# Idle matmuls in TensorE's waits of the front, and two weight units begun early in place of one

## The chip, the cores and the metric

The kernel runs on one core of a Trainium2 chip. The metric is the time of one execution on the device in microseconds (us), as the median of several runs; the profile is of one further execution, with the span of the core's instructions beside its time.

## The reference

For 4 batches and 8 heads, with 576 positions of 64 elements, attention is the sum of two parts: a local one, softmax over the keys within 3 positions, and a dense one between means over 4 neighbouring positions (144 of them), repeated fourfold. The result, as 2304 tokens of 512 elements, goes through two feed-forward layers.

```python
q_d, k_d, v_d = (t.reshape(B, H, Sd, 4, D).mean(axis=3) for t in (q, k, v))
out_up = np.repeat(sm_attn(q_d, k_d, v_d), 4, axis=2)
scores = np.where(np.abs(pos[:, None] - pos[None, :]) < 4, scale * q @ k.T, -1e9)
out_local = softmax(scores) @ v
x = (out_up + out_local).transpose(0, 2, 1, 3).reshape(B * S, H * D)     # 2304 x 512
x = (silu(x @ w_gate) * (x @ w_val)) @ w_out                              # 512 -> 1536 -> 512
h = x @ w2_in                                                             # 512 -> 2048
return (h * clip(h + 3, 0, 6) / 6) @ w2_out                               # 2048 -> 512
```

## The kernel before

The tokens are worked in five blocks (`BLOCKS = [8, 6, 8, 8, 6]`, in units of 64 tokens). The kernel has two stages. In the **front** (to about 65 us) `first_batch` computes the attention of the first batch, whose tokens are block 0 with 64 left over, in five tiles of 122 tokens (the last of 88). A tile i passes through `scores(i)` (TensorE writes `fS`), `norm(i)` (VectorE takes the maxima `fnm`, ScalarE the exponentials `held` with their sums `fsm`, VectorE the reciprocal and the multiply), `trans(i)` (TensorE transposes into `fPT`, ScalarE copies to `turned`) and `values(i)` (TensorE writes `fO`, VectorE adds the dense part on the way out: `fxf`). `put_cols` then splits the tile into a high part (ScalarE) and a low part (VectorE) in `xr`, the moving operand of the feed-forward layers, kept as two fp32r numbers for each value.

From then on, in the **dense** stage, `run_unit` goes through the weight units of each block: G0, G1, V0, V1, G2, G3, V2, V3 and so on, then the products with `w_out` (`aO`), then H and `aP` for the second layer. A unit of kind G, V or H is 12 matmuls of up to 512 columns into a bank `mm`, of which there are two, so that V0 needs the bank of G0, and G2 that of V0. The bank of G0 is read by ScalarE's silu (`sl`); that of V0 by VectorE's product `sl0` (L950), which G2 therefore waits for. Only unit 0 (`HALVES = 1`) is cut in two column ranges, of 244 and 268 columns, so that its first range can run as soon as two tiles are done, between the matmuls of the later tiles.

A weight unit passes through five steps, each started some units ahead (`LR, LD, LA, LB, LS = 8, 6, 5, 4, 3`): `load_raw` (SyncE's queue loads `w64`, four buffers), `decode_a` (ScalarE, `top`), `decode_b` (VectorE, `w32`, three buffers of two units each), `split_unit` for each pair (ScalarE the high part and VectorE the low part of `wr`, three buffers), and in block 0 a write of the decoded pair to memory (`kept`), issued on ScalarE's queue. Blocks 1 to 4 load `kept` into the same buffers as `w32`. In block 0 the attention of the next batches runs on VectorE beside the matmuls: products `pr` of `q` and `k`, reductions, products with `v`, and sums `o`, which TensorE transposes (`px`).

The order on each engine comes from a scheduler that goes by the program's order and its own estimate of when things are ready; instructions under `keep_in_program_order` are held in the order of the code. In the front, matmuls without use (`fill`, L431, 512 columns of zeros) already stand in the waits ahead of the first tiles.

```python
ps = bank("mm", f"p{kind}{bi}_{f}", 2)[:, :nt]
cols = [slice(0, nt)]
if i < HALVES:
    cols = [slice(0, 244), slice(244, nt)]
```

Of the kernel before, what the change touches and what calls it, by code (L numbers as in the profile page):

```python
# [12 lines left out]
BF16 = mybir.dt.bfloat16  # L13
# [8 lines left out]
P = 128  # L22
# [7 lines left out]
CUTS = [[3, 2], [2, 2, 2, 2], [3, 2, 3], [3, 3], []]  # L30
LR, LD, LA, LB, LS = 8, 6, 5, 4, 3
WARM = 14
HALVES = 1
CLOAD = (0, 4)


# [9 lines left out]
def tile_kernel(  # L46
# [12 lines left out]
    nc = tc.nc  # L59
# [9 lines left out]
    NC = DM // P  # L69
# [18 lines left out]
    def bank(tag, name, bufs=1):  # L88
        return pp.tile([P, 512], F32, tag=tag, name=name, bufs=bufs)
# [8 lines left out]
    ident = cp.tile([P, P], F32, name="ident")  # L98
# [169 lines left out]
    def put_cols(bi, col, xv):  # L268

        if bi not in xr:  # L270
            xr[bi] = sp.tile([P, NC, 2, UMAX * UT], F32R, tag="xr", name=f"xr{bi}")
        dst = xr[bi][:, :, :, col:col + xv.shape[2]]
        nc.scalar.activation(dst[:, :, 0], xv, AF.Copy)  # L273
        nc.vector.tensor_tensor(dst[:, :, 1], xv, dst[:, :, 0].bitcast(F32), op=ALU.subtract)
# [42 lines left out]
    def first_batch():  # L317

        QT = 122
# [4 lines left out]
        with tc.tile_pool(name="fp", bufs=1) as fp:  # L324
# [72 lines left out]
            def values_of(i):  # L397
                return vw[i][:, i % 2].rearrange("p (h d) -> p h d", h=H)
# [32 lines left out]
            def fill(ps, n):  # L431

                for _ in range(n):
                    tc.keep_in_program_order(nc.tensor.matmul(ps, idle[:, :P], idle, start=True, stop=True))

            def load_T(w, c):
                src = qn[w, c // 2]
                for th in range(2):
                    tag = ("acc0", "acc1", "acc2")[turn[0] % 3]
                    turn[0] += 1  # L440
                    ps = bank(tag, f"fT{w}{c}{th}")
                    fill(ps, 2)
                    ps = ps[:, :S // 2]
                    for t in range(3):
                        tc.keep_in_program_order(nc.tensor.transpose(
                            ps[:, t * TT:(t + 1) * TT],
                            src[:, 3 * th + t, c % 2 * 2:c % 2 * 2 + 2].rearrange("j h d -> j (h d)"),
                            ident[:TT, :TT],
                        ))
                    if w == "q":  # L450
                        nc.vector.tensor_scalar(
                            qT[:, c, th * S // 2:(th + 1) * S // 2], ps, 0.125, None, op0=ALU.mult
                        )
                    else:
                        nc.scalar.activation(kT[:, c, 3 + th * S // 2:3 + (th + 1) * S // 2], ps, AF.Copy)
# [67 lines left out]
            def size(i):  # L523
                return min(QT, S - QT * i)
# [55 lines left out]
            def trans(i):  # L580
                n = size(i)
                w_ = n + 6
                pT[i] = turned[:WK, i % 2, :NC * 2 * QT].rearrange("p (c a s) -> p c a s", c=NC, a=2)
                for hh in range(2):
                    ps = bank(f"acc{2 + hh}", f"fPT{i}_{hh}")[:, :4 * QT]
                    ps = ps.rearrange("p (c a s) -> p c a s", c=2, a=2)
                    for m in range(4):
                        nc.tensor.transpose(
                            ps[:w_, m // 2, m % 2, :n], pe[i][:n, 2 * hh + m // 2, m % 2, :w_], ident[:n, :n]
                        )  # L590
                    to = pT[i][:w_, 2 * hh:2 * hh + 2, :, :n]
                    nc.scalar.activation(to, ps[:w_, :, :, :n], AF.Copy)

            def values(i):
                n = size(i)
                w_ = n + 6
                t0 = QT * i
                po = bank(("pa", "px")[i % 2], f"fO{i}")[:, :NC * QT].rearrange("p (c s) -> p c s", c=NC)
                for c in range(NC):
                    for par in range(2):  # L600
                        rows = slice(par * D, par * D + D)
                        nc.tensor.matmul(
                            po[rows, c, :n], values_of(i)[:w_, 2 * c + par, :], pT[i][:w_, c, par, :n],
                            start=True, stop=True,
                        )

                xf = sp.tile([P, UMAX * UT], F32, tag="sl", name=f"fxf{i}", bufs=3)[:, :NC * QT]
                xf = xf.rearrange("p (c s) -> p c s", c=NC)[:, :, :n]
                cuts = [0]
                head = -t0 % 4  # L610
                if head:
                    cuts.append(head)
                cuts.append(head + (n - head) // 4 * 4)
                if cuts[-1] < n:
                    cuts.append(n)
                for a, e in zip(cuts, cuts[1:]):
                    j0, m = (t0 + a) // 4, e - a
                    if m % 4 == 0 and (t0 + a) % 4 == 0:
                        nc.vector.tensor_tensor(
                            xf[:, :, a:e].rearrange("p c (j t) -> p c j t", t=4),  # L620
                            po[:, :, a:e].rearrange("p c (j t) -> p c j t", t=4),
                            od[:, :, j0:j0 + m // 4, None].to_broadcast([P, NC, m // 4, 4]), op=ALU.add,
                        )
                    else:
                        nc.vector.tensor_tensor(
                            xf[:, :, a:e], po[:, :, a:e], od[:, :, j0:j0 + 1].to_broadcast([P, NC, m]), op=ALU.add,
                        )
                a = 0
                while a < n:
                    bi = max(m for m in range(NB) if starts[m] * UT <= t0 + a)  # L630
                    e = min(n, starts[bi + 1] * UT - t0)
                    put_cols(bi, t0 + a - starts[bi] * UT, xf[:, :, a:e])
                    a = e
# [21 lines left out]
            down_values(1)  # L655
            next(ahead)
            trans(0)
            down_trans(3)
            down_values(2)
            scores(2)  # L660
            prefetch(5 - LR)
            norm(1)
            down_values(3)
            values(0)
            for i in range(1, NT):
                next(ahead, None)
# [44 lines left out]
    def values_d(po, par, vd, h, pt):  # L711
        for kh in range(2):
            nc.tensor.matmul(  # L713
                po[par * D:par * D + D], vd[:, kh, h, :], pt[:, kh, :], start=kh == 0, stop=kh == 1
            )

    first_batch()


# [204 lines left out]
    def run_unit(i):  # L924
        kind, f, bi = units[i]
        nt = BLOCKS[bi] * UT
        r = split.pop(i)
        if kind in "GVH":
            ps = bank("mm", f"p{kind}{bi}_{f}", 2)[:, :nt]
            x = xr[bi] if kind != "H" else state["x2"]  # L930
            cols = [slice(0, nt)]
            if i < HALVES:
                cols = [slice(0, 244), slice(244, nt)]
            for cs in cols:
                for part in (HIGH, LOW):
                    for c in range(NC):
                        for a, b_ in part:
                            nc.tensor.matmul(  # L938
                                ps[:, cs], r[:, a, c], x[:, c, b_, cs],
                                start=part is HIGH and a == c == 0, stop=part is LOW and c == NC - 1,  # L940
# [17 lines left out]
        else:  # L958
# [12 lines left out]
            for part in (HIGH + LOW,) if last else (HIGH, LOW):  # L971
                for e in range(nb):
                    ps = state["acc"][e]
                    ps = ps[:, :nt] if kind == "O" else ps
# [160 lines left out]
```

## Time and profile before

| | |
|---|---|
| median of 3 runs | 967.26 us (966.04 to 967.92) |
| profiled execution, its own time | 962.81 us |
| its span | 961.0 us |
| mean granted TensorE clock | 0.99 |
| TensorE busy | 934.2 us (97%) |
| VectorE busy | 733.5 us (76%) |
| ScalarE busy | 506.7 us (53%) |
| bytes moved by DMA | 160.79 MB |

The busy share of TensorE is that of both stages together: in the first 77.5 us of the span it is busy for 61.80 us, with a mean granted clock of 0.89, and after that nearly always. A granted clock of 1.00 is 2.4 GHz and one of 0.50 is 1.2 GHz. Times in the rows are microseconds from the start of the span.

### The profile page before, as it was taken

How to read it: one execution, taken by the hardware profiler on the slowest of the kernel's cores; microseconds unless marked ns; L12 is line 12 of the kernel's file. 1: busy time of each engine (PE TensorE's matmuls, PEld its weight loads, DVE VectorE, ACT ScalarE, POOL GpSimd, SP SyncE). 2: the span in 40 equal slices, each digit the busy share in tenths (PEclk: the TensorE clock that was granted, in tenths of full speed). 3: DMA queues.
4: the chain of work that ended last, by engine and by line, in shares of the span. 5: the costliest groups of instructions: out<-in, count | busy, mean ns of one | idle time of the engine just before them, and what ended most of it. 6: DMA issues, size and time to landing. Idle time of an engine off the chain costs nothing.

```text
span 961.0 us, 12930 instructions
## 1 busy us (share of the span) xinstructions
PE 934.2 (97%) x4800; PEld 789.1 (82%) x4800; DVE 733.5 (76%) x1067; ACT 506.7 (53%) x945; POOL 111.0 (12%) x115
## 2 busy tenths in 40 slices
PE   8779999999999999999999999999999999999997
PEld 5567888777799988878888778888888888999996
DVE  7689967799889979999664799996347994445652
ACT  4676667876554577543244764443335444444542
POOL 5742000000053300015410000000000000000000
PEclk9789999999999999999999999999999999999999
DMA  8999999466699823359962212462323223434331
GB/s 207 170 271 316 327 341 351 155 209 226 238 287 270 176 72 108 123 189 237 203 139 96 78 66 85 160 216 90 108 88 105 92 88 112 152 132 132 119 123 33
DMA packets 116339, 160.79 MB, mean 167 GB/s; under 512 B 61868, under 2 KB 83756, under 8 KB 116276
## 3 DMA queue, kind: packets, MB, share of 16 engines
q1 hardware_dynamic: 67892, 131.41, 42.3%
q0 software_dynamic: 43488, 10.72, 11.1%
q10 hardware_dynamic: 4896, 17.83, 4.7%
q8 instruction: 38, 0.62, 0.3%
q14 instruction: 25, 0.20, 0.1%
HBM read 137.29 MB, written 22.54 MB: 166 GB/s over the span
## 4 chain that ended last, share of the span: by engine, by line
PE 83%; DVE 11%; ACT 3%; issue 2%; DMA 1%; SPq 0%; ACTq 0%; DVEq 0%
PE pH L938 17%; PE aP L980 16%; PE pG L938 15%; PE aO L980 15%; PE pV L938 15%; DVE wr L237 2%; DVE pv L809 1%; ACT held L560 1%; PE pS L863 1%; DVE xf L838 1%; DVE h L954 1%; PE pO L713 1%; DMA k<-in_k_dram 1%; DVE pv L813 1%; PE pPT L706 1%
## 5 line engine op out<-in xcount | busy, mean ns | idle before, releaser
L237 DVE TENSOR_TENSOR wr<-w,wr 128x1024 fp32r<-128x1024 f32 x170 | 207.5, 1221 | 121.6 <-ACT wr L236 121.3
L236 ACT ACTIVATE wr<-w 128x1024 fp32r<-128x1024 f32 x170 | 179.7, 1057 | 132.4 <-issue 63.1
L938 PE MATMUL pH<-x,wr 128*128 128x512 f32 (+1 forms) x960 | 212.4, 372 | 0.0
L980 PE MATMUL aP<-wr,gH 128*128 128x512 f32 x864 | 211.4, 395 | 0.3 <-ACT gH L955 0.3
L938 PEld LDWEIGHTS pH<-x,wr 128*128 128x128 f32 x960 | 173.0, 188 | 25.1 <-issue 2.5
L980 PEld LDWEIGHTS aP<-wr,gH 128*128 128x128 f32 x864 | 159.6, 188 | 35.1 <-issue 2.7
L938 PE MATMUL pG<-xr,wr 128*128 128x512 f32 (+3 forms) x732 | 156.5, 368 | 3.8 <-ACT xr L273 3.2
L938 PE MATMUL pV<-xr,wr 128*128 128x512 f32 (+1 forms) x720 | 153.4, 368 | 0.0
L980 PE MATMUL aO<-gV,wr 128*128 128x512 f32 (+1 forms) x720 | 152.7, 368 | 0.0
L938 PEld LDWEIGHTS pG<-xr,wr 128*128 128x128 f32 x732 | 133.4, 190 | 21.4 <-ACT xr L273 3.8
L938 PEld LDWEIGHTS pV<-xr,wr 128*128 128x128 f32 x720 | 130.9, 188 | 16.7
L980 PEld LDWEIGHTS aO<-gV,wr 128*128 128x128 f32 x720 | 130.8, 188 | 16.7
L953 ACT ACTIVATE h<-pH,consts 128x512 f32<-128x512 f32 (+1 forms) x80 | 51.5, 644 | 59.7 <-PE pH L938 59.4
L944 ACT ACTIVATE sl<-pG 128x512 f32<-128x512 f32 (+1 forms) x60 | 33.3, 556 | 72.9 <-PE pG L938 72.8
L955 ACT ACTIVATE gV<-sl 128x512 fp32r<-128x512 f32 (+1 forms) x60 | 35.0, 583 | 65.6 <-DVE sl L950 65.5
L955 ACT ACTIVATE gH<-h 128x512 fp32r<-128x512 f32 (+1 forms) x80 | 46.9, 586 | 32.1 <-DVE h L954 31.8
L954 DVE SCALAR_TENSOR_TENSOR h<-h,pH 128x512 f32<-128x512 f32 (+1 forms) x80 | 50.5, 631 | 14.8 <-ACT h L953 14.2
L772 DVE TENSOR_TENSOR pr<-q,k 128x1792 f32<-128x1792 f32 x27 | 54.5, 2020 | 8.3 <-DMA k<-in_k_dram 8.1
L956 DVE TENSOR_TENSOR gH<-h,gH 128x512 fp32r<-128x512 f32 (+1 forms) x80 | 50.5, 632 | 10.4 <-ACT gH L955 10.0
L214 ACT ACTIVATE top<-w 128x512 f16<-128x512 bf16 x68 | 52.1, 788 | 11.0 <-DMA w<-in_moe_w_out_dram 2.9
L809 DVE TENSOR_TENSOR pv<-sc,v 128x1792 f32<-128x1792 f32 x27 | 54.6, 2022 | 0.5
L775 DVE TENSOR_REDUCE sc<-pr 128x28 f32<-128x1792 f32 x27 | 54.3, 2013 | 0.2
(125 smaller groups left out, 758.4 us busy)
## 6 DMA issues: line engine op xcount, KB each, us to landing
w<-kept SPq DMA_DIRECT2D x136, 512.0 KB
kept<-w ACTq DMA_DIRECT2D x34, 512.0 KB
w<-in_moe_w_out_dram SPq DMA_DIRECT2D x28, 512.0 KB
w<-in_moe_w_in_dram SPq DMA_DIRECT2D x16, 512.0 KB
w<-in_moe_w_gate_dram SPq DMA_DIRECT2D x12, 512.0 KB
w<-in_moe_w_val_dram SPq DMA_DIRECT2D x12, 512.0 KB
out_dram<-os SPq DMA_DIRECT2D x16, 256.0 KB
dnq<-in_q_dram POOLq DMA_DIRECT2D x24, 144.0 KB, 7.4
```

The costliest lines, as they stand in the source:

```text
L214: behind(nc.scalar.activation(halves(top[i % 2], 2, F16)[:, :, 1], h3.bitcast(BF16), AF.Copy))
L236: behind(nc.scalar.activation(r[:, :, 0], s, AF.Copy))
L237: behind(nc.vector.tensor_tensor(r[:, :, 1], s, r[:, :, 0].bitcast(F32), op=ALU.subtract))
L772: nc.vector.tensor_tensor(pr, qt[:, a:a + SUB, None, :].to_broadcast([P, SUB, W, D]), win(kt, a, SUB), op=ALU.mult)
L775: nc.vector.tensor_reduce(sc[:, a:a + SUB], pr, axis=AX.X, op=ALU.add)
L809: nc.vector.tensor_tensor(pr, pe[:, a:a + SUB, :, None].to_broadcast([P, SUB, W, D]), win(vt, a, SUB), op=ALU.mult)
L938: nc.tensor.matmul(ps[:, cs], r[:, a, c], x[:, c, b_, cs], start=part is HIGH and a == c == 0, stop=part is LOW and c == NC - 1,)
L953: nc.scalar.activation(h, ps, AF.Relu, scale=1 / 6, bias=half1[:, 0:1])
L954: nc.vector.scalar_tensor_tensor(h, h, 1.0, ps, op0=ALU.min, op1=ALU.mult)
L955: nc.scalar.activation(g[:, 0, :nt], h, AF.Copy)
L956: nc.vector.tensor_tensor(g[:, 1, :nt], h, g[:, 0, :nt].bitcast(F32), op=ALU.subtract)
L980: nc.tensor.matmul(ps, **one, start=f_ == 0 and a == b_ == 0, stop=f_ == nf - 1 and b_ == 1,)
```

## The change

A new function `fill_late` issues n matmuls of 128x256 bf16 elements, the identity by itself, whose result is not used, into the bank that the next step of the tile writes to. `trans(i)` calls it ahead of its first transposes with 0, 6, 10, 12 and 0, and `values(i)` ahead of its matmuls with 0, 0, 0, 4 and 6: 38 in all. Second, two units (G0 and G1) are cut in column ranges, not one, and the first range has 366 columns (three tiles) in place of 244 (two tiles).

```diff
--- before.py
+++ after.py
@@ -30,7 +30,8 @@
 CUTS = [[3, 2], [2, 2, 2, 2], [3, 2, 3], [3, 3], []]
 LR, LD, LA, LB, LS = 8, 6, 5, 4, 3
 WARM = 14
-HALVES = 1
+FILL_T, FILL_V = (0, 6, 10, 12, 0), (0, 0, 0, 4, 6)
+HALVES = 2
 CLOAD = (0, 4)
 
 
@@ -432,6 +433,14 @@
 
                 for _ in range(n):
                     tc.keep_in_program_order(nc.tensor.matmul(ps, idle[:, :P], idle, start=True, stop=True))
+
+            turner = ident.bitcast(BF16)
+
+            def fill_late(ps, n):
+                for _ in range(n):
+                    tc.keep_in_program_order(
+                        nc.tensor.matmul(ps[:, :2 * P], turner[:, :P], turner, start=True, stop=True)
+                    )
 
             def load_T(w, c):
                 src = qn[w, c // 2]
@@ -582,8 +591,10 @@
                 w_ = n + 6
                 pT[i] = turned[:WK, i % 2, :NC * 2 * QT].rearrange("p (c a s) -> p c a s", c=NC, a=2)
                 for hh in range(2):
-                    ps = bank(f"acc{2 + hh}", f"fPT{i}_{hh}")[:, :4 * QT]
-                    ps = ps.rearrange("p (c a s) -> p c a s", c=2, a=2)
+                    ps = bank(f"acc{2 + hh}", f"fPT{i}_{hh}")
+                    if not hh:
+                        fill_late(ps, FILL_T[i])
+                    ps = ps[:, :4 * QT].rearrange("p (c a s) -> p c a s", c=2, a=2)
                     for m in range(4):
                         nc.tensor.transpose(
                             ps[:w_, m // 2, m % 2, :n], pe[i][:n, 2 * hh + m // 2, m % 2, :w_], ident[:n, :n]
@@ -595,7 +606,9 @@
                 n = size(i)
                 w_ = n + 6
                 t0 = QT * i
-                po = bank(("pa", "px")[i % 2], f"fO{i}")[:, :NC * QT].rearrange("p (c s) -> p c s", c=NC)
+                po = bank(("pa", "px")[i % 2], f"fO{i}")
+                fill_late(po, FILL_V[i])
+                po = po[:, :NC * QT].rearrange("p (c s) -> p c s", c=NC)
                 for c in range(NC):
                     for par in range(2):
                         rows = slice(par * D, par * D + D)
@@ -930,7 +943,7 @@
             x = xr[bi] if kind != "H" else state["x2"]
             cols = [slice(0, nt)]
             if i < HALVES:
-                cols = [slice(0, 244), slice(244, nt)]
+                cols = [slice(0, 366), slice(366, nt)]
             for cs in cols:
                 for part in (HIGH, LOW):
                     for c in range(NC):
```

The scheduler gives another order for this program. The first place is VectorE in the front, tiles 3 and 4: the digit behind a name is the tile, `fnm4` are the maxima of tile 4, `fsm3` the sums of tile 3, `held` the multiply of tile 3, `xr0` the low part of tile 1, `w32` a decode, `fxf2` the addition of tile 2. Before:

```order
L558 TENSOR_REDUCE fnm4_764<-fS4_0_765 88x4
L558 TENSOR_REDUCE fnm4_764<-fS4_1_766 88x4
L569 TENSOR_SCALAR fsm3_697<-fsm3_697 122x8
L570 RECIPROCAL fsm3_697<-fsm3_697 122x8
L571 TENSOR_TENSOR held_229<-held_229,fsm3_697 122x1024
L274 TENSOR_TENSOR xr0_678<-fxf1_742,xr0_678 128x4x122
L223 SCALAR_TENSOR_TENSOR w32_2_726<-w64_3_394,top1_161 128x512
L619 TENSOR_TENSOR fxf2_807<-fO2_798,tmp_262 128x4x120
```

With the change:

```order
L578 TENSOR_SCALAR fsm3_703<-fsm3_703 122x8
L579 RECIPROCAL fsm3_703<-fsm3_703 122x8
L567 TENSOR_REDUCE fnm4_780<-fS4_0_781 88x4
L567 TENSOR_REDUCE fnm4_780<-fS4_1_782 88x4
L275 TENSOR_TENSOR xr0_678<-fxf1_748,xr0_678 128x4x122
L224 SCALAR_TENSOR_TENSOR w32_2_732<-w64_3_394,top1_161 128x512
L580 TENSOR_TENSOR held_229<-held_229,fsm3_703 122x1024
L632 TENSOR_TENSOR fxf2_823<-fO2_814,tmp_262 128x4x120
```

The sums and the reciprocal of tile 3 come ahead of the maxima of tile 4, and the multiply `held` goes behind the `xr0` and the decode.

The second place is VectorE at the dense start, from the low part of the second weight pair (`wr4`) on: `pr1_0` and `sc1_0` are the next batch's first chunk, `sl0_0` is the product of silu(G0) and V0. Before:

```order
L237 TENSOR_TENSOR wr4_929<-w32_4_885,wr4_929 128x2x512
L772 TENSOR_TENSOR pr1_0_0_1087<-q1_0_890,k1_0_892 128x1792
L775 TENSOR_REDUCE sc1_0_1086<-pr1_0_0_1087 128x28
L223 SCALAR_TENSOR_TENSOR w32_6_959<-w64_7_789,top1_161 128x512
L223 SCALAR_TENSOR_TENSOR w32_8_1012<-w64_8_882,top0_159 128x512
L772 TENSOR_TENSOR pr1_0_4_1251<-q1_0_890,k1_0_892 128x1792
L950 TENSOR_TENSOR sl0_0_921<-sl0_0_921,pV0_0_961 128x512
L237 TENSOR_TENSOR wr6_982<-w32_6_959,wr6_982 128x2x512
```

With the change:

```order
L238 TENSOR_TENSOR wr4_967<-w32_4_923,wr4_967 128x2x512
L785 TENSOR_TENSOR pr1_0_0_1137<-q1_0_928,k1_0_930 128x1792
L224 SCALAR_TENSOR_TENSOR w32_6_1009<-w64_7_805,top1_161 128x512
L224 SCALAR_TENSOR_TENSOR w32_8_1062<-w64_8_920,top0_159 128x512
L788 TENSOR_REDUCE sc1_0_1136<-pr1_0_0_1137 128x28
L785 TENSOR_TENSOR pr1_0_4_1301<-q1_0_928,k1_0_930 128x1792
L224 SCALAR_TENSOR_TENSOR w32_8_1062<-w64_9_963,top1_161 128x512
L238 TENSOR_TENSOR wr6_1032<-w32_6_1009,wr6_1032 128x2x512
L963 TENSOR_TENSOR sl0_0_959<-sl0_0_959,pV0_0_1011 128x512
```

The reduction `sc1_0` goes behind two decodes, and a further decode (of raw unit 9) and the subtraction `wr6` stand ahead of `sl0_0`. On ScalarE the silu of G0 comes behind the first decoding steps of raw units 7 and 8 there, and that of G1 behind the write-out `kept3` and the step of unit 9; before, both silus stood ahead of them. On TensorE 3 matmuls of G0's first range stand ahead of `fO3`, where 2 stood ahead of `fO2`, 6 ahead of `fO3` and 1 ahead of `fO4`; the rest of G0 and all of G1 come behind `fO4` in both.

The third place is ScalarE near the end of block 0, around the write-out `kept31`; `h` and `gH` belong to the H units 12 and 13, `wr` and `top` to weight units. Before:

```order
L273 ACTIVATE xr1_875<-xf12_2455 128x4x64
L953 ACTIVATE h0_13_2527<-pH0_13_2513,consts_101 128x512
L955 ACTIVATE gH0_12_2500<-h0_12_2501 128x512
L236 ACTIVATE wr62_2510<-w32_62_2485 128x2x512
L955 ACTIVATE gH0_13_2526<-h0_13_2527 128x512
L229 DMA kept31_156<-w32_62_2485 128x1024
L214 ACTIVATE top1_161<-w64_65_2462 128x512
```

With the change:

```order
L274 ACTIVATE xr1_913<-xf12_2505 128x4x64
L215 ACTIVATE top0_159<-w64_64_2474 128x512
L966 ACTIVATE h0_12_2551<-pH0_12_2537,consts_101 128x512
L237 ACTIVATE wr62_2560<-w32_62_2535 128x2x512
L230 DMA kept31_156<-w32_62_2535 128x1024
L968 ACTIVATE gH0_12_2550<-h0_12_2551 128x512
L966 ACTIVATE h0_13_2577<-pH0_13_2563,consts_101 128x512
L215 ACTIVATE top1_161<-w64_65_2512 128x512
L215 ACTIVATE top0_159<-w64_66_2532 128x512
```

The write-out `kept31` now stands directly behind `wr62`, ahead of `gH0_12` and `h0_13`. In the same stretch TensorE's `px13` stands right behind unit pH14 and no longer behind three matmuls of pH15, and on VectorE the subtraction `wr64` stands ahead of the decode of raw unit 66, with the same set of work ahead of `o`. GpSimd's order is the same, and SyncE's loads stand in the same order up to unit 66.

## Rows read from the trace of the kernel before

**Rows 1.** TensorE by stretch of the span: us, busy (instructions), granted clock, DMA share, GB/s

```profile
49.20:52.40 3.20, 3.18 (x44) 1.00 1.32 253
55.20:58.50 3.30, 3.30 (x23) 0.50 1.35 186
65.50:68.60 3.10, 3.10 (x14) 0.50 1.02 399
77.50:961.00 883.50, 872.37 (x4318) 1.00 0.55 163
```

**Rows 2.** Waits of TensorE after 77.5: line, releaser, us in total, times, longest

```profile
PE px L829 <- DVE o L815: 3.4, 5, 2.4
```

**Rows 3.** Chain of waits into 77.51: start, us, what

```profile
62.02 7.51 DMA k<-in_k_dram
...
76.86 0.61 DVE sl L950
...
77.51 0.50 PE pG L938
```

**Rows 4.** Timeline of TensorE: start, us, instruction, count, [idle before, releaser]

```profile
5.60 0.59 PE L434 MATMUL fTq<-idle 128*128 128x512 bf16 x2
...
49.22 1.10 PE L602 MATMUL fO<-turned,vw 128*64 128x122 f32 x16 [1.97 <-ACT turned L592]
50.25 1.05 PE L588 MATMUL fPT<-ident,held 122*128 122x122 f32 x8
...
55.10 0.72 PE L938 MATMUL pG<-xr,wr 128*128 128x244 f32 x2 [2.70 <-ACT xr L273]
55.74 1.89 PE L602 MATMUL fO<-turned,vw 128*64 128x122 f32 x16
...
71.20 5.71 PE L938 MATMUL pV<-xr,wr 128*128 128x512 f32 x24
```

**Rows 5.** Timeline of VectorE in the front, tiles 2 to 4

```profile
52.74 0.99 DVE L558 TENSOR_REDUCE fnm<-fS 88x4 f32<-88x376 f32 x2
...
54.40 1.22 DVE L571 TENSOR_TENSOR held<-held,fsm 122x1024 f32<-122x1024 f32 x1
55.55 0.66 DVE L274 TENSOR_TENSOR xr<-fxf,xr 128x488 fp32r<-128x488 f32 x1
...
57.68 0.66 DVE L619 TENSOR_TENSOR fxf<-fO,tmp 128x480 f32<-128x480 f32 x1 [0.88 <-PE fO L602]
```

**Rows 6.** Timeline of VectorE at the dense start

```profile
66.32 1.23 DVE L237 TENSOR_TENSOR wr<-w,wr 128x1024 fp32r<-128x1024 f32 x1 [0.50 <-ACT wr L236]
69.64 2.03 DVE L772 TENSOR_TENSOR pr<-q,k 128x1792 f32<-128x1792 f32 x1 [2.10 <-DMA k<-in_k_dram]
...
73.64 1.28 DVE L223 SCALAR_TENSOR_TENSOR w<-w,top 128x512 int32<-128x512 int32 x2
```

**Rows 7.** Timeline of ScalarE, front and dense start

```profile
59.47 1.07 ACT L592 ACTIVATE turned<-fPT 128x488 f32<-128x488 f32 x2
...
67.90 0.60 ACT L944 ACTIVATE sl<-pG 128x512 f32<-128x512 f32 x1
...
71.74 1.41 ACT L214 ACTIVATE top<-w 128x512 f16<-128x512 bf16 x2
...
74.36 1.07 ACT L236 ACTIVATE wr<-w 128x1024 fp32r<-128x1024 f32 x1 [0.96 <-DVE w L223]
```

**Rows 8.** Timeline of TensorE, VectorE and ScalarE's queue around 253.75

```profile
253.75 0.41 PE L829 MATMUL px<-ident,o 128*128 128x128 f32 x2 [2.36 <-DVE o L815]
...
251.45 0.69 DVE L223 SCALAR_TENSOR_TENSOR w<-w,top 128x512 int32<-128x512 int32 x1 [2.09 <-ACT h L953]
...
244.36 0.33 ACTq L229 DMA_DIRECT2D kept<-w  x1
```

**Rows 9.** DMA queue q10 from 242.3 to 248 and 248 to 251.4: packets, MB, share

```profile
q10 hardware_dynamic: 2, 0.00, 0.2%
...
q10 hardware_dynamic: 144, 0.52, 37.7%
```

## The prediction

> **What bounds the kernel now.** I read TensorE's windows first. From 77.50 us to the end of the span it is busy 872.37 of 883.50 us at a granted clock of 1.00 [rows 1]; its longest waits there are 3.4 us in five pieces ahead of `px` [rows 2]. From the dense stage on TensorE is the bound, so the end moves with two things: when the unbroken run of matmuls that begins with unit G2 (77.51) can start, and what happens to the waits behind it. Ahead of 77.51 TensorE waits for others. So I read second the chain of waits into 77.51 [rows 3]: the load of `k` for the next batch lands 7.51 us after its issue at 62.02; VectorE then makes two products, a reduction and two decodes of weights, and behind them `sl`, the product of silu(G0) and V0, which frees the bank that G2 writes to. VectorE had idled 2.10 us for `k` [rows 6]. What happens to TensorE ahead of that is not on the path, unless it moves the issue of `k` or comes later than this cover.
>
> Third, TensorE's clock in the front. After the wait of 2.70 us that ends at 55.10 [rows 4] the granted clock is 0.50 from 55.20 to 58.50, the level of 1.2 GHz, and again from 65.50 to 68.60; after the wait of 1.97 us that ends at 49.22 [rows 4] it is 1.00 until 52.40 [rows 1]. The 16 matmuls of `fO` took 1.10 us at the one level and 1.89 at the other [rows 4].
>
> **The change part by part.**
>
> *The 38 fills.* None has run in this form. The nearest row is the old fill, two of 512 columns in 0.59 us, 0.3 us each at most [rows 4]; by half the columns I take 0.15 us, and 0.3 as the upper end. Ten of them (1.5 us) stand ahead of tile 2's transposes, which followed `fO1` at once at 50.25 [rows 4]. They and the scores of tile 4 come 1.5 us later; VectorE, in its new order, asks for these scores only behind tile 3's reciprocal at 54.4 [rows 5], so that is hidden. Twelve stand between `fO2` (ends at 55.74 + 1.10 = 56.8) and tile 3's transposes: 1.8 us, so these start at 58.6 and end at 59.4, or 60.2 at half clock; ScalarE took them at 59.47 [rows 7]. So it is 0 to 0.7 us late there (2.5 with 0.3 us for each), and with it the rest of the front. The cover is VectorE's 2.10 us of idling for `k`; only at the upper price 0.4 us would come through.
>
> What the fills may win is the half clock at 55.20, 0.79 us of `fO2` [rows 4]. On the path it is worth nothing, since VectorE's order turns around: the multiply `held` of tile 3 now stands behind two reductions (0.99), an `xr` (0.57) and a decode (0.64), and so ends at 55.62 + 2.2 = 57.8 us; the addition that empties `fO2` used to start at 57.68 [rows 5] and starts behind it, at about the same time. Cost of the fills 0; ends -0.8 (if `fO2`'s gain is passed on to the load of `k`) and +0.4.
>
> *The split of G0 and G1.* The columns are the same; G1's 12 matmuls become 24. A matmul of 512 columns takes 5.71/24 = 0.24 us [rows 4] and a shorter one no more, so the extra is 0 to 2.9 us. The cover is ScalarE: silu0, which started at 67.90 behind the table load, now also stands behind two decodes, which took 1.41 us [rows 7]. So silu0 starts at about 69 and V0 at 69.5, whenever G0 is done before 69. Cost 0. Should it miss by a us, V1 still ends before `sl0` is ready.
>
> *The order at the dense start.* Here the change costs. On VectorE `sl0` stood directly behind the second product; now a decode (`w32_8`'s second half) and the subtraction `wr6` stand between. A decode takes 1.28/2 = 0.64 us, such a subtraction 1.23 us [rows 6]: G2 starts at 77.51 + 1.87 = 79.4. Lower end 0, if VectorE came 1.9 us earlier, for which `k` would have to land earlier; upper end more than 1.87 if ScalarE's half of `wr6` is late. That half started at 74.36 [rows 7] and now comes behind silu1 and `qdT`; it may slip by the 1.9 us without being late.
>
> *The clock at the new wait.* silu1 stands on ScalarE behind the write-out `kept3`, which waits for the decode w7 (69.64 + 2.03 + 0.64 = 72.3 [rows 6]), and behind one decode of 0.7: V1 runs from 73.7 to 76.6. Then G2 waits about 2.6 us. That lies between the 1.97 that left the clock up and the 2.70 that was followed by a fall. A fall costs half of 3.3 us [rows 1], 1.65, since TensorE is the bound from there. Both ends, 0 and 1.65, stay open; I take 0, narrowly, since a fall that comes already in the pause of 1.2 us ahead of V1 is hidden.
>
> *The wait at 253.75.* TensorE waited 2.36 us for `o`, and VectorE, just before, 2.09 us to begin the decode w66 [rows 8]. The view names ScalarE's `h`; but this decode writes to the buffer from which `kept31` is written out. That write was issued at 244.36 [rows 8], and its queue (q10) moved next to nothing until 248 and 0.52 MB from there to 251.4 [rows 9]: the wait is for the write. ScalarE's new order issues `kept31` right behind `wr62`, ahead of two `gH` and an `h`, so ahead of the loads that crowded it. Then VectorE's 2.09 us go. `px` now also stands three matmuls (0.71 us) earlier in TensorE's row. With VectorE as late as TensorE the wait left is 2.36 - 2.09 + 0.71 = 0.98, so 1.4 us come back; if VectorE keeps its time (its two pieces of work were brought forward, not added), all 2.36. I take 1.9, between the two; ends 0 and 2.36.
>
> **Sum.** 0 (fills) + 0 (split) + 1.9 (order) + 0 (clock) - 1.9 (write-out) = 0.0 us. It is made against the profiled execution, 962.81 us (span 961.0); the runs' median of 967.26 is 0.46% more, and the change of 0.0 is carried over to it: 967.3 us. 0.2%, about what a measurement of this kernel can tell from no change, is 1.93 us.
>
> The page "DMA: Bandwidth & Descriptors" of the Trainium skill (section "Anatomy of one DMA — SWDGE (gpsimd) path") gives a transfer about 2.0 us and its bytes over 436e3 per us. For `k`, 576 KB, that would be an estimated 3.4 us; the trace shows 7.51 [rows 3].
>
> **The rivals.**
> - *B, the clock falls at G2's wait:* +1.65, 969.0. For it, the fall behind 2.70 us, and a pause ahead of V1 close by; against it, the 1.97 us without one. It decides from the point at which G2 itself runs at half clock.
> - *C, the write-out gives nothing back,* because something else holds `o` (ScalarE's half of `wr64`, whose subtraction now comes ahead of w66 on VectorE): +1.9, 969.2, and with the fall 970.8. Slower. For it: VectorE has the same work ahead of `o` as before. Against it: ScalarE's half of `wr64` was done in the time that VectorE idled.
> - *D, the front's gain is passed on.* If 0.8 us of `fO2` reaches the decode that frees the buffer ahead of the load of `k`, the dense start comes 0.8 us earlier; with all 2.36 back 1.9 - 0.8 - 2.4 = -1.3, 966.0, and with the other 1.0 us of `px` waits gone too -2.3, 965.0. Against it, VectorE's order above.
> - *E, `k` lands on its own size, not on its queue's traffic:* then VectorE begins its product behind `wr4`, at 66.32 + 1.23 = 67.5, and not at 69.64 [rows 6], and the sum is -2.1: 965.2. Against it: the transfers run at 399 GB/s together while `k` is under way [rows 1], and the load stands in the same place in its queue in both orders. It is what the page's rule above would make of `k`.
>
> **How the numbers follow.** A, the forecast (966.2 to 968.4): 0.35. B: 0.29, half of it beyond 0.2%. C: 0.15, four fifths beyond. D: 0.16, three quarters beyond. E: 0.05. So faster 0.12 + 0.05 = 0.17, slower 0.15 + 0.12 = 0.27, same 0.56. The range leaves out the lower end of D and the upper end of C: 965.0 to 970.1.
>
> **What would show it.** Right: `sl` ends near 79.3 and G2 starts at 79.4; the addition of `fO2` still near 57.8, whatever the clock there; `k` landing near 69.6; no wait of VectorE at w66, and a `px` wait at 253 under 1 us. Wrong: a granted clock of 0.50 in the 3 us from G2's start (B); the `px` wait unchanged (C); `k` landing under 69 us (D, E); or tile 3's transposes so late that VectorE no longer idles ahead of its first product.

## The result, and the profile after

The changed kernel took 976.45 us as the median of four runs (975.51 to 978.56); the kernel before took 966.65 beside them (965.94 to 967.92). The ratio is 1.0103 with an interval of 1.0082 to 1.0124: slower by 9.8 us, where no change was forecast.

The profiled execution took 976.88 us (span 975.1, granted clock 0.99), near the runs' median. That of before, 962.81, lies 3.84 us under its runs' median; so the two executions differ by 14.07 us, of which 14.07 - 3.84 - 0.43 = 9.8 us are the difference of the medians. Part of the rest can be placed: in the profile after, `fO1` starts at 52.05, 2.8 us later than before. The first fills that the change adds run at 46.68, and by then the rows were as late already (`fO0` starts at 45.21, before at 42.42). Of these 2.8 us 1.37 are in the first 14 matmuls, which took 4.57 us in the profile of before and 5.94 here; the same 14 took from 4.70 to 6.16 us in the other kernels below. I call the 2.83 us from 49.22 to 52.05 the late start and take it off where the two traces are set against each other.

First TensorE by stretch (us from the span's start, us, busy with its instructions, granted clock, DMA share, GB/s):

```profile
58.00:61.30 3.30, 3.24 (x37) 1.00 1.42 177
68.00:71.10 3.10, 3.10 (x25) 1.00 0.89 291
79.60:84.80 5.20, 5.20 (x13) 0.50 1.10 383
85.30:90.70 5.40, 5.40 (x26) 1.00 1.16 338
```

In this profile the clock of the front is up: 1.00 where before had 0.50, at `fO2` and at the second range of G0 [rows 1]. A new fall stands at 79.60 to 84.80. The waits of TensorE from 77.5 on (line, releaser, us in total, times, longest):

```profile
PE pV L951 <- ACT sl L957: 7.1, 2, 4.0
PE px L842 <- DVE o L828: 2.9, 4, 1.7
```

Before, the only large group there was `px` with 3.4 us [rows 2]. Now V units wait for ScalarE's silu (`sl`), 7.1 us in two waits. TensorE's timeline (start, us, instruction, count, [idle before, releaser]) shows both:

```profile
52.05 1.10 PE L615 MATMUL fO<-turned,vw 128*64 128x122 f32 x16 [1.97 <-ACT turned L603]
53.09 1.27 PE L442 MATMUL fPT<-ident 128*128 128x256 bf16 x10
...
58.06 1.10 PE L615 MATMUL fO<-turned,vw 128*64 128x122 f32 x16 [1.77 <-ACT turned L603]
59.09 1.48 PE L442 MATMUL fPT<-ident 128*128 128x256 bf16 x12
...
72.47 2.99 PE L951 MATMUL pV<-xr,wr 128*128 128x512 f32 x12
79.50 5.49 PE L951 MATMUL pV<-xr,wr 128*128 128x512 f32 x12 [4.03 <-ACT sl L957]
...
85.21 5.76 PE L951 MATMUL pG<-xr,wr 128*128 128x512 f32 x24
...
91.03 3.00 PE L951 MATMUL pV<-xr,wr 128*128 128x512 f32 x12
97.11 3.06 PE L951 MATMUL pV<-xr,wr 128*128 128x512 f32 x12 [3.08 <-ACT sl L957]
```

Ten fills took 1.27 us and twelve 1.48, 0.12 to 0.13 each; `fO2`, at 58.06, took 1.10 us instead of 1.89. V0 starts at 72.47: 1.27 us after before's 71.20 [rows 4], or 1.56 ahead of it without the late start. Up to here this execution wins 1.6 us; the experiments do not bear out that it wins them by the fills (see "The fills at 0" below). Then V1 waits 4.03 us and runs at half clock, 5.49 us for 12 matmuls instead of 2.99, and V3 waits 3.08. ScalarE's rows tell why (ACTq is the engine issuing a DMA):

```profile
70.14 1.28 ACT L957 ACT_TABLE_LOAD   x1
71.43 0.60 ACT L957 ACTIVATE sl<-pG 128x512 f32<-128x512 f32 x1
75.97 0.39 ACTq L230 DMA_DIRECT2D kept<-w  x1
78.23 0.78 ACT L215 ACTIVATE top<-w 128x512 f16<-128x512 bf16 x1 [6.20 <-DMA w<-in_moe_w_out_dram]
78.88 0.56 ACT L957 ACTIVATE sl<-pG 128x512 f32<-128x512 f32 x1
...
94.19 0.78 ACT L215 ACTIVATE top<-w 128x512 f16<-128x512 bf16 x1 [5.30 <-DMA w<-in_moe_w_val_dram]
95.84 0.77 ACT L215 ACTIVATE top<-w 128x512 f16<-128x512 bf16 x1 [0.88 <-DMA w<-in_moe_w_out_dram]
...
96.49 0.57 ACT L957 ACTIVATE sl<-pG 128x512 f32<-128x512 f32 x1
```

silu1, which V1 needs, is the row at 78.88. It stands behind the write-out `kept3` (75.97) and behind the decode of raw unit 9. The 6.20 us of idling that the view puts down to that unit's load are two waits: until 75.97 for the decode w7, whose result `kept3` writes out, and only from 76.36 on for the load. That load was issued on SyncE's queue at 65.52, behind those of `k` and `v`, and its decode could start 12.7 us later. silu3 (96.49) stands behind the decodes of units 13 and 14, which wait for their loads. VectorE's rows:

```profile
60.09 0.65 DVE L632 TENSOR_TENSOR fxf<-fO,tmp 128x480 f32<-128x480 f32 x1
...
73.31 2.03 DVE L785 TENSOR_TENSOR pr<-q,k 128x1792 f32<-128x1792 f32 x1 [3.24 <-DMA k<-in_k_dram]
...
80.45 0.68 DVE L224 SCALAR_TENSOR_TENSOR w<-w,top 128x512 int32<-128x512 int32 x1
81.05 1.22 DVE L238 TENSOR_TENSOR wr<-w,wr 128x1024 fp32r<-128x1024 f32 x1
82.19 0.68 DVE L963 TENSOR_TENSOR sl<-sl,pV 128x512 f32<-128x512 f32 x1
```

The addition of `fO2` is at 60.09, 57.26 without the late start; before it was at 57.68 [rows 5]. The load of `k` took 8.7 us from its issue at 64.51, against 7.51 before [rows 3], and VectorE's product starts behind it at 73.31. `sl0` is indeed behind the decode and `wr6`, at 82.19, but G2 no longer waits for it: V1 ends later still. Near 253.75 [rows 8] the third place of the change reads so on TensorE and ScalarE:

```profile
262.43 0.41 PE L842 MATMUL px<-ident,o 128*128 128x128 f32 x2
```

```profile
251.99 0.33 ACTq L230 DMA_DIRECT2D kept<-w  x1
252.11 1.05 ACT L237 ACTIVATE wr<-w 128x1024 fp32r<-128x1024 f32 x1
253.30 0.64 ACT L968 ACTIVATE gH<-h 128x512 fp32r<-128x512 f32 x1
```

`kept31` is issued ahead of `gH`, and the wait of 2.36 us is gone. What each stretch added, by the start of the same work in both traces:

| place | before | after | later by |
|---|---|---|---|
| `fO1` | 49.22 | 52.05 | 2.83 |
| V0 | 71.20 | 72.47 | 1.27 |
| G2 | 77.51 | 85.21 | 7.70 |
| first `aO` | 89.10 | 100.23 | 11.13 |
| an `aO` in the middle of block 0 | 154.49 | 166.09 | 11.60 |
| first `aP` behind that `px` | 256.08 | 265.44 | 9.36 |
| an `aP` in block 1 | 421.36 | 435.44 | 14.08 |
| end | 961.0 | 975.1 | 14.1 |

From V0 to G2 the change loses 6.4 us: the wait of 4.03 and 2.5 of half clock, less small gains. From G2 to `aO` it loses 3.4, of which 3.08 are V3's wait. At `px` it gets 2.2 back. From there to 421.36 it loses 4.7, of which four waits make 0.67 + 0.55 + 0.65 + 1.71 = 3.58 against one of 0.41 before (0.65 and 1.71 are for `px`); the other 1.5 is in no single row.

### The profile page after: what moved, and what is told of

Same layout as the page of the kernel before. It is cut to its first block, busy times and chain, and to the rows that moved or that the text cites. A ratio compares the mean times of both kernels' runs of the same rounds, so it can differ in the third digit from the quotient of the medians.

```text
span 975.1 us, 13038 instructions
## 1 busy us (share of the span) xinstructions
PE 941.9 (97%) x4848; PEld 792.8 (81%) x4850; DVE 734.0 (75%) x1067; ACT 505.0 (52%) x945; POOL 109.1 (11%) x115
## 4 chain that ended last, share of the span: by engine, by line
PE 79%; DVE 9%; DMA 5%; ACT 3%; issue 2%; SPq 0%; ACTq 0%; DVEq 0%
PE pH L951 18%; PE aP L993 18%; PE aO L993 13%; PE pV L951 12%; PE pG L951 12%; DMA k<-in_k_dram 3%; DVE wr L238 2%; DMA w<-in_moe_w_out_dram 1%; ACT held L569 1%; PE pS L876 1%; PE pO L726 1%; DMA w<-in_moe_w_gate_dram 1%; DVE xf L851 1%; PE pPT L719 1%; PE px L842 1%
## 5 line engine op out<-in xcount | busy, mean ns | idle before, releaser
L951 PE MATMUL pV<-xr,wr 128*128 128x512 f32 (+1 forms) x720 | 156.9, 373 | 7.1 <-ACT sl L957 7.1
```

What stands on the lines that cost most here:

```text
L951: nc.tensor.matmul(ps[:, cs], r[:, a, c], x[:, c, b_, cs], start=part is HIGH and a == c == 0, stop=part is LOW and c == NC - 1,)
```

## The experiments

The theory after the result (O in what follows): the loss is the order that the scheduler chose on ScalarE, not the matmuls that the change adds. Its rivals: the fills or the cut cost something themselves; the late load of `k` costs it; the clock does. The order was changed by one helper, which puts an instruction behind another of the same engine in the schedule without any wait of its own:

```
def hold(ins, key):   # ins is scheduled behind the instruction marks[key]
    tc.add_manual_dep(ins.ins, marks[key].ins.name,
                      DependencyInfo(NoSync, DATA), reason=key)
```

The kernels ran in three groups of four, each on one chip beside the kernel before: e1 to e4 (before 967.59 us), e5 to e8 (968.15) and e9 to e12 (967.72). Ratios are to these runs of the kernel before, with an interval behind them; a ratio is not the quotient of the two medians (for e5 that would be 0.9977, and the ratio is 0.9993). Each median is followed by its lowest and highest run. The edits are shown shortened.

**e1, the fills alone.** The cut is taken back.

```diff
-HALVES = 2
+HALVES = 1
-cols = [slice(0, 366), slice(366, nt)]
+cols = [slice(0, 244), slice(244, nt)]
```

> The fills without the new cut (one unit cut at column 244, as before). Theory O (order): the loss of the change is in ScalarE's queue, where the silu of G1 (and of G3) stands behind decodes that wait for their loads, and the fills cost next to nothing themselves. In this kernel's order silu1 stands behind the write-out kept3 but ahead of the decode of unit 9, and silu3 behind the decodes of units 11 and 12 alone: V1 should wait 1 to 2 us, not 4.0, and the time be 968 to 971 us. Theory W (work): the added matmuls make the front late; then most of the loss is here, 973 us or more, with V0 starting over 1 us later than before and no long wait of V1 for silu.

Measured: 972.48 us (969.70 to 979.45), ratio 1.0057 (1.0028 to 1.0085). The scheduler gives a third order: `kept3` ahead of silu1, but no decode of unit 9 between. TensorE's timeline, then ScalarE's silu1:

```profile
75.48 3.02 PE L951 MATMUL pV<-xr,wr 128*128 128x512 f32 x12 [1.24 <-ACT sl L957]
...
79.48 3.02 PE L951 MATMUL pG<-xr,wr 128*128 128x512 f32 x12 [0.72 <-DVE sl L963]
83.43 3.06 PE L951 MATMUL pG<-xr,wr 128*128 128x512 f32 x12 [0.93 <-DVE sl L963]
```

```profile
74.83 0.60 ACT L957 ACTIVATE sl<-pG 128x512 f32<-128x512 f32 x1 [3.67 <-DVE w L224]
```

V1 waits 1.24 us for a silu that stands behind `kept3`, for which ScalarE idles 3.67 us. Smaller waits follow at G2, G3 and later silus. The time lies between the two expectations, 1.5 us over O's and 0.5 under W's. V0 starts at 71.25, as before (71.20), so the lost time is not in the front, where W put it; but this run alone doesn't clear the fills.

**e2, the cut alone.** All fills are 0.

```diff
-FILL_T, FILL_V = (0, 6, 10, 12, 0), (0, 0, 0, 4, 6)
+FILL_T, FILL_V = (0,) * 5, (0,) * 5
```

> The new cut (two units, columns 0 to 366) without the fills. Theory O: silu1 stands behind kept3 but ahead of the decode of unit 9, and the subtraction wr6 stands ahead of sl0: V1 waits 1 to 2 us, G2 another 1 us, silu3 behind one decode: 968 to 972 us. Theory W: the twelve more matmuls behind the last tile are the loss: 973 us or more, with the end of the G block after 71.5 us and V0 late because of it.

Measured: 969.73 us (967.15 to 972.08), ratio 1.0021 (1.0005 to 1.0036). The time is as O has it, the waits are not: V1 does not wait at all. Here the silus are in time, but `wr6` stands ahead of `sl0`:

```profile
72.46 5.72 PE L951 MATMUL pV<-xr,wr 128*128 128x512 f32 x24
...
80.21 5.75 PE L951 MATMUL pG<-xr,wr 128*128 128x512 f32 x24 [1.78 <-DVE sl L963]
```

V0 and V1 run as one, and G2 waits 1.78 us for `sl0`, where before it waited 0.60. From V0 to G2 it is 7.75 us, 1.44 more than before. This is one half of the step that the prediction put at 1.87: of its two instructions only `wr6` (1.22 us) stands ahead of `sl0` here, the decode does not.

**e3, the whole change with the silus held first.** The decodes of units 7 to 10 stand behind silu1, those of 11 and 12 behind silu3.

```diff
+if 7 <= i <= 12: hold(ins, "sl1" if i < 11 else "sl3")   # decode_a
+marks[f"sl{f}"] = nc.scalar.activation(sl, ps, AF.Silu)
```

> The whole change, but on ScalarE the first decoding steps of units 7 to 10 are ordered behind silu1, and those of units 11 and 12 behind silu3; no work is added or left out. Theory O: V1's wait of 4.0 us and V3's of 3.1 us are gone, the time is 965.5 to 968 us, that of the kernel before. Theory W: nothing comes back, 974 to 977 us.

Measured: 972.46 us (970.37 to 974.97), ratio 1.0047 (1.0027 to 1.0067). Missed. The waits of V1 and V3 are gone as expected, but the scheduler, with the new times, put `sl0` on VectorE behind the second reduction as well. TensorE, then VectorE:

```profile
71.69 5.71 PE L961 MATMUL pV<-xr,wr 128*128 128x512 f32 x24
...
82.34 7.14 PE L961 MATMUL pG<-xr,wr 128*128 128x512 f32 x24 [4.68 <-DVE sl L973]
```

```profile
73.50 2.02 DVE L795 TENSOR_TENSOR pr<-q,k 128x1792 f32<-128x1792 f32 x1 [4.13 <-DMA k<-in_k_dram]
...
79.67 2.02 DVE L798 TENSOR_REDUCE sc<-pr 128x28 f32<-128x1792 f32 x1
81.61 0.68 DVE L973 TENSOR_TENSOR sl<-sl,pV 128x512 f32<-128x512 f32 x1
```

The wait has moved to another engine: G2 waits 4.68 us for `sl0` and then runs its 24 matmuls in 7.14 us instead of 5.76. Holding one engine's order is no test of the fills as long as the scheduler is free on the other.

**e4, the next batch's loads two units later,** a test of the load of `k` as the cause.

```diff
-CLOAD = (0, 4)
+CLOAD = (2, 4)
```

> The whole change, with the loads of the next batch's first q, k and v issued two units later, behind the raw loads of units 9 and 10. ScalarE's order keeps silu1 behind the decode of unit 9. Theory O: the raw load of unit 9 lands at about 71 us and not 78, so V1 waits under 1.5 us; k lands 2 to 3 us later, which VectorE feels, so the sum is less than the 7 us of the two waits: 968 to 973 us. Theory W: V1 starts as late as with the whole change, near 79 us, and the time stays at 975 us or more.

Measured: 976.46 us (973.53 to 976.88), ratio 1.0081 (1.0060 to 1.0102). V1 didn't wait, as expected, since the weights' loads came first. The sum was missed: now `k` is so late that VectorE's first product starts at 81.15 after a wait of 7.20, and `sl0` stands behind it.

```profile
71.69 5.71 PE L951 MATMUL pV<-xr,wr 128*128 128x512 f32 x24
...
86.36 7.57 PE L951 MATMUL pG<-xr,wr 128*128 128x512 f32 x24 [8.70 <-DVE sl L963]
```

The trade is between the same two loads: whichever comes second holds an engine on whose queue work for TensorE stands behind it.

**e5, the whole change with both orders held.** As e3, and on VectorE the first reduction, the decode of unit 9 and `wr6` stand behind `sl0`.

```diff
+if i == 9: hold(ins, "h0")                 # decode_b; h0 is the product sl0
+if i == 6: hold(ins, "h0")                 # split_unit, the subtraction wr6
+if (b, c, a) == (1, 0, 0): hold(ins, "h0") # the reduction sc1_0
```

> The whole change with the order of two engines held: on ScalarE the first decoding steps of units 7 to 10 behind silu1 and those of 11 and 12 behind silu3, and on VectorE the product sl0 ahead of the first reduction, of the decode of unit 9 and of wr6. Theory O (the order of ScalarE and VectorE at the dense start is the loss): no wait of TensorE over 1 us between V0 and the second pair of V units, 965 to 969 us. Theory W (the added matmuls have a price of their own): still 970 us or more, with the lost time ahead of V0.

Measured: 965.92 us (963.70 to 968.59), ratio 0.9993 (0.9974 to 1.0013). As expected, but for one wait a little over 1 us:

```profile
71.71 5.72 PE L969 MATMUL pV<-xr,wr 128*128 128x512 f32 x24
...
77.48 2.99 PE L969 MATMUL pG<-xr,wr 128*128 128x512 f32 x12
81.65 3.06 PE L969 MATMUL pG<-xr,wr 128*128 128x512 f32 x12 [1.18 <-DVE sl L981]
```

V0, V1 and G2 run as one; only G3 waits, 1.18 us. With every matmul of the change in place and the order of two engines held, the whole loss is gone.

**e6, the kernel before with the same orders held:** e5 without fills and cut.

> The kernel before, without fills and without the new cut, with the same order held as in the run with the product first. Theory O: within 0.3% of that run and of the kernel before, 964 to 968 us; its wait of 0.6 us for sl0 is gone. Theory W: at least 3 us faster than the same order with fills and cut.

Measured: 965.68 us (963.59 to 967.76), ratio 0.9969 (0.9949 to 0.9988). As expected. The medians of e5 and e6 are 0.24 us apart, well within the spread of either: fills and cut together neither cost nor win anything that these runs can tell.

**e7, the matmuls of before with the change's place of silu1:** no fills, no new cut; silu1 is put behind the decode of unit 9, and units 1 to 3 are handed to the scheduler later, so that it can be.

```diff
+marks[f"top{i}"] = ins                 # decode_a
+if i == 1: hold(ins, "top9")           # silu
-run_unit(i)
+for j in {1: (), 4: (1, 2, 3, 4)}.get(i, () if i in (2, 3) else (i,)): run_unit(j)
```

> The kernel before, without fills and without the new cut, but with silu1 held behind the first decoding step of unit 9 on ScalarE (units 1 to 3 are therefore written down later in the program, and wr6 comes ahead of sl0). Theory O: V1 waits 3 to 5 us for silu1, which waits for the load of unit 9, and the clock may fall behind it: 971 to 976 us, most of the loss of the change. Theory W: under 969 us, since no matmul was added.

Measured: 969.10 us (967.99 to 972.21), ratio 1.0008 (0.9988 to 1.0028). The mechanism came, the size was missed:

```profile
70.97 2.89 PE L947 MATMUL pV<-xr,wr 128*128 128x512 f32 x12
...
78.70 4.49 PE L947 MATMUL pV<-xr,wr 128*128 128x512 f32 x12 [4.59 <-ACT sl L953]
83.03 5.60 PE L947 MATMUL pG<-xr,wr 128*128 128x512 f32 x24
```

V1 waits 4.59 us and its 12 matmuls take 4.49, and G2 starts at 83.03, 5.5 us later than before, of which 1.57 are a late start of this execution (`fO1` at 50.79). But here the order near 253 also turned so that the `px` wait is gone, which gives 2.3 us back, and the silus of V2 and V3 are in time. Against the kernel before, then, no loss can be told. Against e6, its neighbour on the same chip without any of the waits, e7 loses 3.4 us, and the runs of the two don't overlap.

**e8, the fills alone, orders held:** e5 with the cut of before.

> The 38 fills with one unit cut at column 244 as before, and the same order held as in the run with the product first. Theory O: the same as that run, 965 to 969 us. Theory W, with the fills as the cause: 969 us or more, against under 967 us for the same order without fills.

Measured: 964.79 us (963.87 to 966.92), ratio 0.9971 (0.9952 to 0.9989): better than the kernel before and the changed one, and 0.9 us under e6, which has no fills; an interval for this difference, from the runs resampled, is -2.0 to +0.7, so the two are not told apart. The time lies 0.2 us under O's range and 4 under W's: the fills cost nothing here.

**e9, e8 with the write-out first too:** `kept31` is issued as soon as its decode is done, and the `h` of unit H13 stands behind it.

```diff
+if i == 63: marks["kept31"] = nc.scalar.dma_start(kept[31], t)  # decode_b
+if i == 59: hold(ins, "kept31")                                 # h
```

> The 38 fills, one unit cut at column 244, the order of the dense start held (silus and sl0 first), and near the end of block 0 the write-out kept31 issued as soon as its pair is decoded, ahead of h of unit 13; VectorE's order then has o ahead of the decode of unit 66. If TensorE's wait of 2.2 us for px near 253 comes from that write-out, it is gone: 962.3 to 964 us, 0.3 to 0.5% faster than the kernel before. If the wait has another cause, or the time saved is lost in block 1, 964.5 to 966 us as without this edit.

Measured: 964.84 us (963.14 to 969.63), ratio 0.9975 (0.9957 to 0.9992). Missed: the wait of 2.2 us at 253 is gone, but nothing of it is left in the time beside e8 (from another group, on another chip). Two waits for `px` of 0.49 and 1.70 us stand in block 1, and e8 has the like (0.65 and 1.70) beside its wait at 253. TensorE from V0 on is unbroken:

```profile
71.40 5.72 PE L972 MATMUL pV<-xr,wr 128*128 128x512 f32 x24
...
77.18 5.80 PE L972 MATMUL pG<-xr,wr 128*128 128x512 f32 x24
```

**e10, e9 without the fills.**

> The same two orders held, without fills and with the cut of the kernel before. If the fills are worth nothing on the path: the same time as with them, 962.3 to 964.5 us. If the clock that they keep up is worth something: 0.7 to 1.5 us slower than with them.

Measured: 966.64 us (963.62 to 969.24), ratio 0.9986 (0.9966 to 1.0006). e9 is 1.8 us under it, with an interval of -3.6 to +0.4. It lies above both expectations. By the medians of the two pairs, e8 with e6 and e9 with e10, the fills are worth 0.9 and 1.8 us once the order is held, but both intervals include zero.

**e11, the change with the decode of unit 9 alone held behind silu1.**

```diff
+if i in (9,): hold(ins, "sl1")
```

> The whole change, and on ScalarE only the first decoding step of unit 9 held behind silu1 (the write-out kept3 stays ahead of silu1; silu3 then stands behind the step of unit 12 but no longer behind 13 and 14). VectorE keeps wr6 ahead of sl0. If the two silus are the loss: V1's wait falls from 4.0 to 1 or 2 us and V3's 3.1 us is gone, G2 still waits about 2 us for sl0: 968 to 971 us. If not: 974 us or more.

Measured: 981.93 us (980.12 to 983.18), ratio 1.0150 (1.0122 to 1.0178). Missed by far. The scheduler put the decode of unit 10 in that place instead:

```profile
70.12 0.60 ACT L967 ACTIVATE sl<-pG 128x512 f32<-128x512 f32 x1
...
79.24 0.78 ACT L222 ACTIVATE top<-w 128x512 f16<-128x512 bf16 x1 [8.52 <-DMA w<-in_moe_w_gate_dram]
79.89 0.57 ACT L967 ACTIVATE sl<-pG 128x512 f32<-128x512 f32 x1
```

ScalarE idles 8.52 us ahead of it, first at `kept3`, then for its load; silu1 comes at 79.89, V1 waits 6.01, and two later silus cost 2.02 and 2.73. It is the same kind of wait with a load that lands later, and a larger loss.

**e12, the change with the decodes of units 11 to 14 held behind silu3.**

```diff
+if i in (11, 12, 13, 14): hold(ins, "sl3")
```

> The whole change, and on ScalarE only the first decoding steps of units 11 to 14 held behind silu3; silu1 stays behind that of unit 9. V1's wait of 4.0 us and the half clock behind it stay, V3's 3.1 us is gone: 972 to 974 us, against 976.5 with the whole change. If V3's wait is only passed on to a later stage: 975 us or more.

Measured: 971.47 us (969.83 to 976.40), ratio 1.0050 (1.0031 to 1.0069), half a us under the expected range, with the waits as expected:

```profile
79.44 5.49 PE L961 MATMUL pV<-xr,wr 128*128 128x512 f32 x12 [4.28 <-ACT sl L967]
...
85.15 5.94 PE L961 MATMUL pG<-xr,wr 128*128 128x512 f32 x24
...
91.15 5.72 PE L961 MATMUL pV<-xr,wr 128*128 128x512 f32 x24
```

V1's wait (4.28) and half clock stay, V2 and V3 run as one. Against the whole change (1.0103) this takes off half a per cent, some 5 us. Gone in the profile are V3's wait of 3.08 us and the two of 0.67 and 0.55 in block 1; that these two follow from the first is not shown. What is left of e12, 971.47 - 967.72 = 3.75 us, would be V1's part if nothing else differed; the 3.4 of e7 against e6 is near it.

## Why the prediction was wrong

**The step that failed** is the one on the clock at the new wait: "silu1 stands on ScalarE behind the write-out `kept3`, which waits for the decode w7 (69.64 + 2.03 + 0.64 = 72.3 [rows 6]), and behind one decode of 0.7: V1 runs from 73.7 to 76.6." The place was right, and so was its start: V0 was put at 69.5 and came at 72.47 - 2.83 = 69.64. But the decode of unit 9 was priced by its 0.7 us of work, not by when its input is there. Without the late start the pieces are: `k` at 70.48, put at 69.6, so 0.9 late; `kept3` at 75.97 - 2.83 = 73.14, put at 72.3, with the same two durations (73.31 + 2.03 + 0.64 = 75.98 in the trace); then the decode at 78.23 - 2.83 = 75.40, 1.9 us after the queue was free for it at 75.97 + 0.39 - 2.83 = 73.53, because its load landed only then. V1's wait was put at 1.2 us and was 4.03; 0.9 of the difference is `k`, 1.9 the load.

**The same step stopped too early.** The order was followed to silu1 and G2 and no further. silu3 stands behind decodes of units 13 and 14 in the same way, 3.08 us, and by e12 some 5 of the 9.8 us go with this half, more than with the first. No rival named a wait of a V unit for a silu; B had the right kind of loss (a longer wait, then half clock) at the wrong unit. D and E need `k` to land early, and it came 0.9 us late; C needs the wait at 253 to stay, and it is gone.

**The clock.** A fall at G2 was left open, between 0 and 1.65 us. It fell at V1, behind 4.03 us, and took 2.5 us: 12 matmuls at 5.49 instead of 2.99. G2 ran at 1.00. The bracket by which the step judged, a wait of 1.97 us without a fall and one of 2.70 with it, does not hold in the other profiles: at the same place, `fO1`, waits of 1.96 and 1.97 us were followed by a fall in e5, e7 and e12 (the 16 matmuls took 1.80, 1.56 and 1.86 us and not 1.10), and V3's wait of 3.08 us was not (granted clock 1.00, 3.06 us). At G2, which did not wait, the bracket was not put to the test.

**The order on VectorE, 1.87 us.** Right as a step: in the trace after, the decode and `wr6` take 82.19 - 80.45 = 1.74 us ahead of `sl0`. Wrong as a term of the sum: in the whole change it is hidden, since V1 is later still. e2 shows one half of it on the path, 1.44 us.

**The fills at 0.** Right in the sum: they cost 0.12 us each (0.15 was taken), and with the order held (e5, e6, e8) they can't be told from nothing. But what they win in the front is not shown. They did not always hold the clock up: in e4 and e11, with all 38 fills, `fO2` ran at 0.50 again, as in this row of e4:

```profile
56.41 1.89 PE L615 MATMUL fO<-turned,vw 128*64 128x122 f32 x16 [2.14 <-ACT turned L603]
```

And the 1.6 us up to V0 are no more than executions differ by. From `fO1` to V0 it is 21.98 us before and 20.42 after; without fills it is 20.50 in e6, 20.18 in e7 and 21.64 in e10, with them from 20.09 (e9) to 21.88 (e11). In e6 and e7 the second range of G0 and G1 ran at full clock without any fill (24 matmuls in 4.49 us in e6, 6.06 before).

**The split at 0.** Right: e2 has V0 at 72.46 and V1 without a wait, and e5, with the cut, equals e6 and e8 within their spread.

**The wait at 253.75, -1.9.** Right in the profile: no wait of VectorE or TensorE there, and the lag falls from 11.60 to 9.36. Missed was that it doesn't last. In all ten kernels of this study without that wait, the changed one among them, a wait of 1.68 to 1.71 us for `px` stands some 90 us later, in block 1, where before, e5 and e6, which keep their 2.3 us at 253, have 0.41 to 0.89. That would leave some 0.3 to 1 us of the term. It is a coincidence of rows and no more: e8 has both waits, and no run changed the second alone.

**Still open.** What makes the wait of 1.7 us in block 1, and the 1.5 us there that are in no row, was not isolated. And e6 is 2.5 us under the kernel before though the profile of before shows only 0.6 us between V1 and G2; that `sl0` no longer stands behind the load of `k` in those executions where that lands later would give it, but this is argued, not shown. The clock of the front, which differs between profiles with the same work there, is another candidate.

## What to carry to other kernels

G1 was done by 72.4 here, and its silu ran at 78.88, because ScalarE stood at the write-out and the decode ahead of it. In such a queue an instruction that is moved ahead costs what its input is late, not what it takes; so for each one that a new order puts in front, read when its load lands, and follow the order through every later consumer of that engine (here both silus, not the first). An edit that only adds idle work to one engine can turn the order on the others, as e1 shows: with a scheduler, hold the few instructions that the bound engine waits for, on every engine at once, and only then judge the edit. The version to keep is one with silus and `sl0` held first: e8, with the fills (964.79 us, ratio 0.9971, interval 0.9952 to 0.9989), or e6, without them (965.68 us, 0.9969, 0.9949 to 0.9988). How much of the 0.3% is the held order alone is not settled, since e10, with that order and no fills, has 0.9986 (0.9966 to 1.0006).

## What the runs showed of the hardware

The load of `k`, 576 KB behind the same neighbours in its queue, took 7.51 us before, 8.7 after, and from 6.6 (e6) to 9.3 (e5) in the other kernels that issue the loads in this order (all but e4). The page "DMA: Bandwidth & Descriptors" of the Trainium skill (section "Anatomy of one DMA — SWDGE (gpsimd) path") gives a fit for loads that GpSimd issues (the prediction took it for any transfer), by which this size would take an estimated 3.4 us. This load is issued by SyncE, with others under way beside it, so the longer times here are no test of the fit.

The 14 matmuls at the very start took 4.57 to 6.16 us between executions, and `fO1` started between 49.22 (before) and 52.66 us (e10), 3.4 us apart in kernels with the same work ahead of it. So one profile is not to be set against another there without lining them up.

The waits of 4.03 (after), 4.68 (e3) and 4.59 us (e7) were each followed by matmuls that took 5.49, 7.14 and 4.49 us (2.99, 5.76 and 2.99 for as many at full clock), those of 1.78 (e2) and 3.08 us (V3 after) by matmuls at their usual time (5.75 and 3.06). The shorter waits at `fO1` and `fO2` went either way: 1.96 us (e5) was followed by a fall, 1.97 (before) was not. In these runs the length of the wait alone does not tell whether the clock falls.
